# Sliding-window attention with V gathered for blocks of eight tokens, weights turned by DMA, and x loaded again in the new row order

## The chip, the cores and the metric

The kernel runs on one core of one Trainium2 chip. The metric is the device time of one execution in microseconds. A core has a matrix engine (TensorE, PE in the profile; its weight loads are PEld), a vector engine (VectorE, DVE), a scalar engine (ScalarE, ACT), GpSimd (POOL), and SyncE (SP), which here does nothing but issue DMAs. Each engine runs its own list of instructions in order; semaphores tie them together.

## The reference

One transformer block with adaptive layernorm on 2048 tokens of width 512 in bf16: attention over a dilated sliding window, then a gated FFN.

```python
mod = (silu(c) @ w_mod).reshape(1, 6, 1, -1)       # sa, ca, ga, sb, cb, gb
h = layernorm(x) * (1 + ca) + sa
x = x + ga * A(h, A_wqkv, A_wo)
h = layernorm(x) * (1 + cb) + sb
x = x + gb * B(h, B_w1, B_w3, B_w2)

def A(x, wqkv, wo):                                # S = 2048, D = 512, H = 32 heads of 16
    q, k, v = split(x @ wqkv)
    idx = arange(S)[:, None] - 2 * arange(8)[None, :]       # W = 8 keys, dilation 2
    logits = einsum('bhsd,bhswd->bhsw', q, k[idx]) * 16 ** -0.5   # idx < 0: -1e9
    o = einsum('bhsw,bhswd->bhsd', softmax(logits), v[idx])
    return o @ wo

def B(x, w1, w3, w2):                              # F = 1792
    return (silu(x @ w1) * (x @ w3)) @ w2
```

## The kernel before

The tokens are 16 tiles T of 128. A small program (`Program`) collects operations with their engine, what they read and write, and a key; two lists written into the file, `ORDER` and `SLOTS`, give the order of all operations and the buffer of every value. `place` splits the order into one list for each engine, `synchronize` works out the semaphores, `emit` writes the instructions. So each engine's order, SP's too, is fixed by `ORDER`, whose numbers count the calls of `p.op` and `p.dma` as `_build` makes them.

What is done, with the lines of the profile:

- Layernorm 1 in groups of tiles (0,1), (2,3), (4-7), (8-11), (12-15) on VectorE (L555, L576). The normalized tiles are turned by TensorE (L636) or, for the last two groups, by DMA (`sb_h<-sb_xn`), and scaled on ScalarE (L644, L621). Then q and k (L691) and v (L711) are projected. V is written to DRAM (`v_scratch_dram<-sb_v`) with its columns ordered by (channel, head).
- The modulation: `gate(0)` and `gate(1)` (L531, from `wm_g`) make ga and gb, which are multiplied into wo (L946) and w2 (L952).
- Attention in seven blocks of pairs of tiles (`BLOCKS`; the last has two pairs). `logits`: VectorE multiplies q with the eight shifted views of k (L742, called pq here), TensorE sums over the 16 channels of each head (L752, four column tiles of 32 at a time; tile 0 gets a mask, L749). `shift`, `exps`, `softmax`: maximum, subtraction, exponential, sum, reciprocal and scaling (L764, L769, L782, L794, L796, L797). The weights then have heads on the partitions. `turn` (L807) transposes them on TensorE into PSUM, and ScalarE copies them to SBUF (L811, `sb_al`), so that (token, offset) pairs lie on the partitions.
- `values`, for one tile: four DMAs of 256 KB copy V from DRAM so that partition 8 t + w of a copy holds the row of V of token t at offset w. Each row of V is so read eight times. VectorE multiplies the copy with the weights in place (L827, one instruction of 4096 elements a partition), TensorE sums over the eight offsets (L855), ScalarE copies the sum to SBUF (L861, `sb_ac`), a DMA transposes it (`sb_ot<-sb_ac`), TensorE multiplies with wo (L867), and VectorE adds the residual x (L871).
- The FFN in groups (0,1), (2,3), (4-7), (8-11), (12,13), (14,15). Layernorm 2 on GpSimd and ScalarE (L586 to L601), the turn by TensorE for the first two groups and by DMA for the others, then w1 and w3 (L883), silu (L889), the product (L892), w2 (L921; L909 for tiles 14 and 15), the last residual (L931) and the store (`out_dram<-sb_o`).

The FFN of one group runs between the attention of later pairs, in the order that the list gives.

Of the kernel before, what the change touches and what calls it, by code (L numbers as in the profile page):

```python
# [73 lines left out]
class Program:  # L74
# [41 lines left out]
    def dma(self, out, in_, key, packets, r=(), w=(), part=(), after=(), eng="sp", cost=450, group=None, transpose=False,  # L116
            store=False, again=False, lat=None):
# [11 lines left out]
        o = self.op(eng, fn, cost, key, r=r, w=w, part=part, after=after, dma=(each, ns, *(lat if lat else (900, 200) if store else (900, 500) if transpose else (1300, 600))))  # L129
# [119 lines left out]
C_PQ, C_RED, C_ACC = 2203, 455, 800  # L249
# [3 lines left out]
def c_mm(n):  # L253
    return n * 5 // 12 + 3

# [13 lines left out]
AC_OLD = ()  # L269
# [3 lines left out]
def _build(p, A_x, A_wqkv, A_wo, B_w1, B_w3, B_w2, c, w_mod, out):  # L273
# [4 lines left out]
    x_view = x2d.rearrange("(t p) d -> p t d", p=P)  # L278

# [10 lines left out]
    qb = [sb([P, KT, 512], bf, f"q{i}") for i in range(4)]  # L290
# [3 lines left out]
    vshb = [sb([P, 8, D], bf, f"vsh{i}") for i in range(2)]  # L294
    pqb = [sb([P, W, KT, P], bf, f"pq{i}") for i in range(2)]
    NSM = 3
    atb = [sb([P, 2, 32, W], bf, f"attn{i}") for i in range(NSM)]
    alb = [sb([P, 2, 8, H], bf, f"al{i}") for i in range(3)]
    mxb = [sb([P, 2, 32], f32, f"mx{i}") for i in range(NSM)]
    ssb = [sb([P, 2, 32], f32, f"ssum{i}") for i in range(NSM)]  # L300
    otb = [sb([P, KT, P], bf, f"ot{i}") for i in range(3)]
# [5 lines left out]
    ones = sb([P, 256], bf, "ones")  # L307
    ind = sb([P, 16], bf, "ind")
    ind2 = sb([P, 2, 32], bf, "ind2")
    before = sb([P, W, 2, 16], bf, "before")  # L310
# [26 lines left out]
    osb = [nc.alloc_sbuf_tensor_at(f"sb_o{i}", [P, D], bf, offset=nc.lookup_mloc(wqkv).addr + 8192 + 1024 * i) for i in range(4)]  # L337
    vsh_x = nc.alloc_sbuf_tensor_at("sb_vshx", [P, 8, D], bf, offset=nc.lookup_mloc(wqkv).addr)
# [12 lines left out]
    vshpool = Pool("vsh", vshb)  # L351
    pqpool = Pool("pq", pqb)
# [8 lines left out]
    def held(pool, items):  # L361

        vals = []
        for i, item in enumerate(items):
# [5 lines left out]
    qkv_hold = held(vshpool, [vsh_x]) + held(opool, osb)  # L370

    vind2 = Val("ind2")
# [16 lines left out]
                                           pattern=[[-W, 16]], channel_multiplier=1), 200, k, w=[vind])  # L389
    p.op("pool", lambda e: e.affine_select(out=ind[:], in_=ind[:], compare_op=ALU.is_ge, fill=0.0, base=W - 1,  # L390
                                           pattern=[[W, 16]], channel_multiplier=-1), 200, k, w=[vind])
    p.op("dve", lambda e: e.memset(ind2[:], 0.0), 80, k, w=[vind2])
    for y in range(2):
        p.op("dve", lambda e, y=y: e.tensor_copy(bass.AP(ind2, 33 * y, [[64, P], [2, 16]]), ind[:]), 150, k, r=[vind], w=[vind2])
    p.op("pool", lambda e: e.memset(before[:], 0.0), 250, k, w=[vbefore])
    p.op("pool", lambda e: e.affine_select(out=before[:], in_=before[:], compare_op=ALU.is_ge, fill=BEFORE, base=0,
                                           pattern=[[-DIL, W], [1, 2], [2, 16]], channel_multiplier=0), 400, k, w=[vbefore])
# [115 lines left out]
    def warm(i, after=()):  # L513

        vw = Val("ps_warm", psum)

        def mm(e):
            return e.matmul(bank(vw)[:, 0:256], ones[:, 0:P], ones[:], start=True, stop=True)

        p.op("pe", mm, 214, ("warm", i), r=[vc], w=[vw], after=after)  # L520
# [210 lines left out]
    def logits(Ts):  # L731

        vl = Val("ps_l", psum)
        for i, T in enumerate(Ts):
# [11 lines left out]
            def red(e, i=i, T=T, vp=vp):  # L746
                c0 = vl.at * 512 + i * W * 32
                if T == 0:
                    e.matmul(PALL[0:32, c0:c0 + W * 32], ones[:, 0:32], before[:], start=True, stop=False, tile_position=(0, 0))  # L749
                for ft in range(KT):  # L750
# [187 lines left out]
    for gi, Ts in enumerate(LN1):  # L938
# [4 lines left out]
        for i, T in enumerate(Ts):  # L943
            proj_v(T, i, vh)
# [10 lines left out]
    for groups in BLOCKS:  # L955
        vls = [logits(Ts) for Ts in groups]
        ves = [shift(Ts, vl) for Ts, vl in zip(groups, vls)]
        for Ts, vl, ve, vx_ in zip(groups, vls, ves, exps(groups, vls, ves)):
            val = softmax(Ts, vl, ve, vx_)
            for i, T in enumerate(Ts):  # L960
                values(T, i, val)
# [114 lines left out]
```

## Time and profile before

| | |
|---|---|
| median of 3 timed runs | 243.23 us (242.37 to 243.58) |
| the profiled execution | 242.82 us, span 241.1 us |
| granted TensorE clock | 1.00 |
| TensorE, VectorE, ScalarE, GpSimd busy | 230.4, 179.6, 138.7, 30.9 us |
| DMA | 38.85 MB in 46317 packets, of which the 64 copies of V 16.8 MB |
| issues on SP | 64 for V, 36 transposes, 18 output stores, 16 stores of v, the rest weights and x |

The span is what the profile covers; the 1.7 us between it and the execution's time lie around it. "Busy" counts a TensorE instruction until its modelled end, which overlaps the next one, so the start-to-start time of a run of matmuls says more than the mean of one. In the timeline a bracket at the end of a line is the idle time of that engine just before, and what ended it.

### The profile page before, as it was taken

The page shows a single profiled execution, that of the slowest core. Times are in us where ns is not written, and L with a number is a line of the kernel's source. Part 1 is how long each engine was busy: PE and PEld are TensorE (multiplying, and loading weights), DVE is VectorE, ACT ScalarE, POOL GpSimd, SP SyncE. Part 2 cuts the span into 40 slices and gives each one's busy share as a digit, 9 for nine tenths or more (in the row PEclk, how much of TensorE's full clock was granted, in tenths as well). Part 3 has the DMA queues.
Part 4 walks back from the last instruction along what each step waited for, and adds up shares of the span by engine and source line. Part 5 has one row for each costly group of instructions (what it writes and reads, how often), then busy time and mean ns, then how long its engine had stood idle before and what let it go on. Part 6 is the DMA issues. An engine that isn't in the chain of part 4 may idle for free.

```text
span 241.1 us, 4538 instructions
## 1 busy us (share of the span) xinstructions
PE 230.4 (96%) x1781; PEld 136.8 (57%) x1806; DVE 179.6 (75%) x279; ACT 138.7 (58%) x267; POOL 30.9 (13%) x66
## 2 busy tenths in 40 slices
PE   7988999979999999999799999999999999999995
PEld 4856454544587685564345444444565584485874
DVE  5697999979989999898999999764565044423542
ACT  2296497688999744955964578646537253140300
POOL 4332060004001000250005301001001000000000
PEclk9999999999999999999999999999999999999999
DMA  6999999999979996693893882253220300000103
GB/s 222 370 327 327 163 262 234 287 282 343 331 134 253 283 270 115 160 272 99 213 256 119 195 197 46 66 141 98 76 79 0 46 0 0 3 22 0 48 0 109
DMA packets 46317, 38.85 MB, mean 161 GB/s; under 512 B 21704, under 2 KB 37080, under 8 KB 46296
## 3 DMA queue, kind: packets, MB, share of 16 engines
q1 hardware_dynamic: 46288, 38.56, 62.5%
q8 instruction: 14, 0.23, 0.4%
q14 instruction: 7, 0.06, 0.1%
q10 hardware_dynamic: 8, 0.00, 0.0%
HBM read 29.62 MB, written 4.21 MB: 140 GB/s over the span
## 4 chain that ended last, share of the span: by engine, by line
PE 50%; ACT 1%; DMA 1%; issue 1%; DVE 0%; SPq 0%
PE pall L883 30%; PE pall L921 12%; PE pall L867 3%; PE pall L909 3%; DMA sb_h<-sb_xn 1%; ACT sb_h L621 1%; PE pall L855 1%; PE pall L752 1%; PE pall L807 0%; ACT sb_al L811 0%; DVE sb_o L931 0%; SPq L124 0%
## 5 line engine op out<-in xcount | busy, mean ns | idle before, releaser
L883 PE MATMUL pall<-sb_h,sb_w 128*128 128x256 bf16 (+1 forms) x665 | 101.8, 307 | 1.0 <-ACT sb_h L621 0.6
L883 PEld LDWEIGHTS pall<-sb_h,sb_w 128*128 128x128 bf16 x672 | 64.8, 98 | 36.2 <-issue 1.5
L892 DVE TENSOR_TENSOR sb_hh<-sb_sg,pall 128x256 bf16<-128x256 bf16 (+1 forms) x84 | 40.4, 505 | 32.1 <-PE pall L883 32.0
L889 ACT ACTIVATE sb_sg<-pall 128x256 bf16<-128x256 f32 (+1 forms) x84 | 36.2, 455 | 43.4 <-PE pall L883 37.3
L921 PE MATMUL pall<-sb_w,sb_hh 128*128 128x512 bf16 x189 | 43.7, 379 | 0.4
L742 DVE TENSOR_TENSOR sb_pq<-sb_q,sb_kT 128x4096 bf16<-128x4096 bf16 x16 | 36.3, 2282 | 0.0
L921 PEld LDWEIGHTS pall<-sb_w,sb_hh 128*128 128x128 bf16 x196 | 19.1, 98 | 21.0
L691 PE MATMUL pall<-sb_h,sb_wqkv 128*128 128x512 bf16 (+1 forms) x159 | 30.3, 336 | 0.1
L827 DVE TENSOR_TENSOR sb_vsh<-sb_vsh,sb_al 128x4096 bf16<-128x4096 bf16 x12 | 27.3, 2286 | 2.4 <-ACT sb_al L811 2.2
L621 ACT ACTIVATE sb_h<-sb_h,sb_modc 128x512 bf16<-128x512 bf16 (+1 forms) x24 | 16.3, 733 | 13.0 <-DMA sb_h<-sb_xn 13.0
L691 PEld LDWEIGHTS pall<-sb_h,sb_wqkv 128*128 128x128 bf16 x160 | 15.1, 98 | 12.2 <-ACT sb_h L644 0.5
L931 DVE TENSOR_TENSOR sb_o<-pall,sb_x 128x512 bf16<-128x512 f32 (+1 forms) x18 | 10.9, 627 | 11.8 <-PE pall L921 8.7
L586 POOL TENSOR_SCALAR sb_nm<-sb_sx 128x2 f32<-128x2 f32 x8 | 3.7, 465 | 115.9 <-DVE sb_x L871 115.9
L590 ACT ACTIVATE sb_xn<-sb_x,sb_nm 128x512 bf16<-128x512 bf16 x16 | 11.4, 714 | 11.7 <-POOL sb_nm L586 11.7
L867 PE MATMUL pall<-sb_wo,sb_ot 128*128 128x512 bf16 x60 | 15.0, 379 | 1.1 <-DMA sb_ot<-sb_ac 0.5
L711 PE MATMUL pall<-sb_wqkv,sb_h 128*128 128x512 bf16 x58 | 15.0, 379 | 0.3 <-issue 0.2
L644 ACT ACTIVATE sb_h<-pall,sb_modc 128x256 bf16<-128x256 bf16 (+1 forms) x18 | 9.9, 616 | 8.6 <-DVE sb_modc L509 6.7
L601 ACT ACTIVATE sb_xn<-sb_x,sb_nb,sb_rs 128x512 bf16<-128x512 bf16 x16 | 12.6, 806 | 3.7 <-POOL sb_nb L599 3.7
L871 DVE SCALAR_TENSOR_TENSOR sb_x<-pall,sb_x 128x512 bf16<-128x512 f32 x16 | 11.0, 688 | 2.3 <-PE pall L867 2.3
L701 ACT ACTIVATE sb_kT<-pall 128x512 bf16<-128x512 f32 x16 | 9.6, 606 | 4.7 <-PE pall L691 4.7
L555 DVE BATCH_NORM_STATS2 sb_st<-sb_x 128x6 f32<-128x512 bf16 x16 | 10.4, 678 | 1.3 <-DMA sb_x<-in_A_x_dram 1.3
L721 ACT ACTIVATE sb_v<-pall 128x512 bf16<-128x512 f32 x16 | 9.6, 612 | 2.4 <-DMA v_scratch_dram<-sb_v 2.3
(87 smaller groups left out, 208.6 us busy)
## 6 DMA issues: line engine op xcount, KB each, us to landing
sb_vsh<-v_scratch_dram SPq DMA_DIRECT2D x48, 256.0 KB, 4.6
sb_vshx<-v_scratch_dram SPq DMA_DIRECT2D x16, 256.0 KB, 4.3
sb_w<-in_B_w_dram SPq DMA_DIRECT2D x6, 512.0 KB, 5.6
sb_w<-in_B_w_dram SPq DMA_DIRECT2D x6, 384.0 KB, 6.0
v_scratch_dram<-sb_v SPq DMA_DIRECT2D x16, 128.0 KB, 5.9
out_dram<-sb_o SPq DMA_DIRECT2D x14, 128.0 KB, 1.9
sb_wqkv<-in_A_wqkv_dram SPq DMA_DIRECT2D x6, 256.0 KB, 6.0
sb_x<-in_A_x_dram SPq DMA_DIRECT2D x4, 256.0 KB, 6.3
```

Of the source, the lines that this page charges most:

```text
L590: p.op("act", lambda e, vn=vn, T=T: e.activation(vn.at[:], x_sb[:, T, :], ACT.Square, bias=nm[:, T, :], accum_out=var[:, T, :]), c_act(512 ...
L601: p.op("act", lambda e, vn=vn, T=T: e.activation(vn.at[:], x_sb[:, T, :], ACT.Identity, bias=nb[:, T, :], scale=rs[:, NT + T, :]), c_act(5 ...
L621: return e.activation(vh.at[:, ft, 0:n * P], vh.at[:, ft, 0:n * P], ACT.Identity, bias=modc[:, 8 * which + ft:8 * which + ft + 1], scale=m ...
L691: ins = e.matmul(bank(vp)[:, j * n:(j + 1) * n], wqkv[:, t, col:col + P], vh.at[:, t, 0:n], start=(t == ORDER[0] and j == 0), stop=(t == O ...
L711: ins = e.matmul(bank(vp), vh.at[:, t, tt * P:(tt + 1) * P], wqkv[:, t, 2 * D:3 * D], start=(t == ORDER[0]), stop=(t == ORDER[-1]))
L742: return e.tensor_tensor(vp.at[:], in0, in1, ALU.mult)
L827: return e.tensor_tensor(v_w, v_w, a_w, ALU.mult)
L867: ins = e.matmul(bank(vy), vt.at[:, ft, :], wo[:, ft, :], start=(ft == 0), stop=(ft == KT - 1))
L883: ins = e.matmul(bank(vp)[:, 0:n], wt[:, t, fi * P:(fi + 1) * P], vh.at[:, t, 0:n], start=(t == 0), stop=(t == KT - 1))
L889: p.op("act", lambda e: e.activation(vt.at[:, 0:n], bank(vgp)[:, 0:n], ACT.Silu), c_act(n), k, r=[vgp], w=[vt], table="silu")
L892: p.op("dve", lambda e: e.tensor_tensor(vh_.at[:, 0:n], vt.at[:, 0:n], bank(vup)[:, 0:n], ALU.mult), c_dve(n), k, r=[vt, vup], w=[vh_])
L921: ins = e.matmul(bank(vz), vhh[fi].at[:, tt * P:(tt + 1) * P], w2[:, fi, :], start=(fi == 0), stop=(fi == NF - 1))
```

## The change

The pairs of tiles are treated as one. The 256 tokens of a pair are 32 blocks of eight. The window of a token reaches back in steps of two, so the eight tokens of a block and their eight offsets need 22 rows of V, which five copies (`s`) of two neighbouring slots for four offsets (32 blocks x 4 offsets on the partitions) hold; each slot of a copy serves one token with its near four offsets and another with its far four. Five DMAs of 256 KB a pair take the place of eight. For this the logits are laid out with heads and the token's place in half a block (`q`) on the partitions, the scaling of the weights (`norm`) is written in two instructions, a DMA transpose takes the place of TensorE's turn and ScalarE's copy (`AT_PE` is empty), and the products are three instructions for 6, 2 and 8 slots, the first into a buffer of its own (`av`).

The sums come out with the tokens of a pair in another order: partition 32 q + j of half z is token 8 j + 4 z + q. So x is loaded a second time in that order, by 16 DMAs in two groups (`AGAIN`) over the rows that layernorm 1 has read; layernorm 2 and the FFN work on the new order, and each output tile is stored by four DMAs of 32 rows, or, for tiles 14 and 15, by one DMA for half the columns whose DRAM side has the dimensions 4, 32, 256. The three buffers of V copies for a tile become two for a pair; q has three buffers for four; the output has six buffers for four. `ORDER` and `SLOTS` are new as a whole.

```diff
+NQB = 3
+AT_PE = ()
+AGAIN = [[0, 1, 2, 3], [4, 5, 6, 7]]
+    def rows(t, T, x, n_pairs, c0=0, n=D):
+        first = T // 2 * 2 * P + T % 2 * 4 + x
+        return bass.AP(t.tensor, t.offset + first * D + c0, [[8 * D, 32]] + ([[2 * P * D, n_pairs]] if n_pairs > 1 else []) + [[1, n]])
...
-    vshb = [sb([P, 8, D], bf, f"vsh{i}") for i in range(2)]
+    vshb = [sb([P, 10, D], bf, f"vsh{i}") for i in range(2)]
+    avb = [sb([P, 6, D], bf, "av0")]
...
             def red(e, i=i, T=T, vp=vp):
+                def group(q):
+                    return PALL[32 * q:32 * q + 32, vl.at * 512:vl.at * 512 + 512].rearrange("p (w n r) -> p w n r", w=W, n=2)[:, :, i, :]
...
-                        ins = e.matmul(PALL[32 * q:32 * q + 32, c0:c0 + W * 32], E_sb[:, ft, :], bass.AP(vp.at, ft * P + 32 * q, [[W * KT * P, P], [KT * P, W], [1, 2], [2, 16]]),
-                                       start=(ft == 0 and (T > 0 or q > 0)), stop=(ft == KT - 1), tile_position=(0, 32 * q))
+                        ins = e.matmul(group(q), E_sb[:, ft, :], bass.AP(vp.at, ft * P + q, [[W * KT * P, P], [KT * P, W], [4, 32]]),
+                                       start=(ft == 0), stop=(ft == KT - 1), tile_position=(0, 32 * q))
...
-        p.op("dve", lambda e: e.tensor_tensor(ve.at[0][:, 0:n], bass.AP(PALL, bank(vl).offset, [[8 * 512, P], [W * 32, n], [1, 32], [32, W]]),
-                                              bass.AP(ve.at[2], 0, [[64, P], [32, n], [1, 32], [0, W]]), ALU.mult),
+        for y in range(2):
+            def norm(e, y=y):
+                return e.tensor_tensor(bass.AP(ve.at[0], y * P, [[512, P], [256, 2], [4, 32], [1, 4]]),
+                                       bass.AP(PALL, bank(vl).offset + y, [[8 * 512, P], [64, 2], [2, 32], [128, 4]]),
+                                       bass.AP(ve.at[2], y, [[64, P], [0, 2], [2, 32], [0, 4]]), ALU.mult)
+            p.op("dve", norm, 74 + 267, k, r=[vr, vx_], part=[va], hold=[ve, vl], lock=False)
+        val = Val("al", alpool)
+        if Ts[0] not in AT_PE:
+            p.dma(lambda: val.at[:], lambda: ve.at[0][:], ("at", Ts[0]), (128, 1024), r=[va], w=[val], hold=[ve], cost=1270, transpose=True)
+            return val
...
-        for q in range(4):
-            p.dma(lambda q=q: vv.at[:, 2 * q:2 * q + 2, :],
-                  bass.AP(v_dram, (PAD + T * P + 32 * q) * D, [[2 * D, 16], [-DIL * D, W], [1, 2 * D]]), ("vl", T), (128, 2048),
+        for s in range(5):
+            p.dma(lambda s=s: vv.at[:, 2 * s:2 * s + 2, :],
+                  bass.AP(v_dram, (PAD + T0 * P - DIL + 2 * s) * D, [[8 * D, 32], [-2 * DIL * D, 4], [1, 2 * D]]), ("vl", T0), (128, 2048),
...
-        avs[T] = p.op("dve", av, C_PQ, ("av", T), r=[val], w=[vv], lock=True)
+        first = p.op("dve", av(1, 2, 6, 2, vpr, 0), c_av(6), k, r=[val, vin], w=[vhigh], hold=[vv, vpr], lock=True)
+        p.op("dve", av(1, 0, 2, 0, vv, 0), c_av(2), k, r=[val, vin], part=[vlow], hold=[vv], lock=True)
+        o = p.op("dve", av(0, 0, 8, 2, vv, 2), c_av(8), k, r=[val, vin], part=[vlow], hold=[vv, vpr], lock=True)
...
+        if T >= NT - 2:
+            first = T // 2 * 2 * P + T % 2 * 4
+            finals.append(p.dma(bass.AP(out2d.tensor, out2d.offset + first * D + c0, [[D, 4], [8 * D, 32], [1, n]]), lambda: vo.at[:, 0:n], ("zo", T), (128, 2 * n),
+                                r=[vo], cost=400, store=True))
+            return
+        parts = []
+        for x in range(4):
+            finals.append(p.dma(rows(out2d, T, x, 1, c0, n), lambda x=x: vo.at[32 * x:32 * x + 32, 0:n], ("zo", T), (32, 2 * n), r=[vo], cost=400, store=True, group=parts))
...
+    for g, prs in enumerate(AGAIN):
+        loads = []
+        for z in range(2):
+            Ts = [2 * pr + z for pr in prs]
+            for x in range(4):
+                p.dma(x_sb[32 * x:32 * x + 32, Ts[0]:Ts[-1] + 1:2, :], rows(x2d, Ts[0], x, len(Ts)), ("again", g), (32 * len(Ts), 1024),
+                      part=[vx[T] for T in Ts], group=loads, cost=500)
```

Numbering the operations gives the lists in words. SP from the first store of v to the second output transpose ("vl" a copy of V, "st" a store of v, "hT" a transpose for sb_h, "OT" one for sb_ot, "AT" the one of the weights, "X" a load of x of the first group, "w" a weight):

```
before: st1 st0 w hT8 st2 hT10 w vl0 hT9 hT11 vl0 vl0 vl0 st3 vl1 vl1 vl1 st4 vl1 w hT14 hT12 st6 w st11 hT13 hT15 w w OT0 OT1
after:  X st3 st1 X st0 hT8 hT9 w X hT10 hT11 st7 vl0 hT14 vl0 vl0 vl0 vl0 st6 AT0 w st2 w st5 hT13 w X hT15 hT12 X X OT1 X OT0 (then X)
```

VectorE between the reciprocal and the first products of the first pair: before, xn12, xn13, the scaling, pq3, xn15; after, a copy for the modulation, the two halves of the scaling, xn12, xn13, pq2, xn15. TensorE ahead of the first gate and between the gates: before, three transposed pieces of tiles 4 to 7, gate 0, the other pieces and three projections, gate 1; after, all eight pieces, gate 0, eight projections, gate 1. The projection of v of tile 12 lies ahead of the first FFN matmul before, and behind it after.

## The prediction

> **What bounds the kernel now.** I read the page first: busy shares and the 40 slices.
>
> ```profile
> PE 230.4 (96%) x1781; PEld 136.8 (57%) x1806; DVE 179.6 (75%) x279; ACT 138.7 (58%) x267; POOL 30.9 (13%) x66
> PE   7988999979999999999799999999999999999995
> DVE  5697999979989999898999999764565044423542
> DMA  6999999999979996693893882253220300000103
> ```
>
> TensorE is busy almost throughout, VectorE for some 125 us in the middle, the DMA engines for the first 70 us. Busy time overstates TensorE, so the second view is the chain that ended last, in order of time.
>
> ```profile
> 110.83 2.44 DMA sb_h<-sb_xn
> 113.29 2.94 ACT sb_h L621 x4
> 116.50 5.99 PE pall L883 x27
> 232.34 6.13 PE pall L909 x56
> 238.49 0.42 DVE sb_o L931
> ```
>
> (Most of its pieces are left out.) From 116.5 us to the end everything on the chain is TensorE at its issue rate (56 matmuls of 256 columns in 6.13 us, 109 ns each). Behind 116.5 us only TensorE work counts; ahead of it TensorE waits for data. So the third view is TensorE's timeline up to there, for its gaps and for what fills it while the first pair of tiles passes through attention.
>
> ```profile
> 18.10 0.54 PE L531 MATMUL pall<-sb_csT_bf,sb_wm_g 128*128 128x1 bf16 x16 [0.63 <-DMA sb_wm_g<-in_w_mod_dram]
> 22.71 0.54 PE L531 MATMUL pall<-sb_csT_bf,sb_wm_g 128*128 128x1 bf16 x16 [0.88 <-DMA sb_wm_g<-in_w_mod_dram]
> 36.77 0.39 PE L807 MATMUL pall<-sb_ident,sb_attn 128*128 128x128 bf16 x4
> 50.99 1.67 PE L867 MATMUL pall<-sb_wo,sb_ot 128*128 128x512 bf16 x7 [0.46 <-ACT sb_h L621]
> 62.20 1.89 PE L691 MATMUL pall<-sb_h,sb_wqkv 128*128 128x512 bf16 x8
> 63.93 1.47 PE L883 MATMUL pall<-sb_h,sb_w 128*128 128x256 bf16 x12
> ```
>
> The last projection (L691) ends just as the first FFN matmul (L883, 63.93 us) can start. Up to there the projections are the only filler; when they are used up, TensorE waits for the first pair's chain: weights (L797), turn (L807), copy (L811), products (L827), column sums (L855), output transpose by DMA, WO (L867), residual (L871), second layernorm, FFN. A delay in this chain that the filler doesn't cover is a delay of the end.
>
> **The change, part by part.** All sums are against the profiled execution, 242.82 us (span 241.1 and 1.7 around it); the median of the timed runs, 243.23, is 0.4 above it, and runs spread from 242.37 to 243.58. About 0.5%, 1.2 us, is what a measurement can tell from no change.
>
> *TensorE.* The turn goes: four transposes take 0.22 us of the queue (the next piece starts at 37.00 after 36.77), eight groups 1.8 us. Two groups lie ahead of the first FFN matmul, six (1.3 us) behind it. The logit and column-sum matmuls keep their number and columns. The mask for tile 0 becomes four matmuls of 32 columns in place of one of 256: under 0.1 us either way.
>
> *ScalarE, GpSimd, buffers.* Eight copies of the turned weights go (L811, 598 ns): 4.8 us on an engine that is 58% busy; what counts is the wait ahead of the products, below. GpSimd builds the mask in five instructions for two (0.2 to 0.6 us each), before tile 0 needs it at 29 us: nothing. Three q buffers for four: the fourth chunk is written from some 50 us on, when the first chunk's last product (at 36.20 us now) is over: nothing.
>
> *VectorE.* The scaling L797 is split in two, the products of a pair become three instructions for two. Four 256-column L892 in a row took 1.41 us, so one adds 0.33; two L797 in a row took 1.22, so one of 512 adds 0.54 to 0.61. Two halves cost about 0.09 more than one; an extra instruction's fixed part, by the same two rows, is 0.08. Eight pairs: 8 x 0.17 = 1.4 us on an engine that is full from 30 to 155 us. After that it idles and TensorE has a stock of FFN work, so I cost this at nothing on the end; if the third FFN group (116.5 us) waits for it, half of it, 0.7 us, shows.
>
> *DMA and SP.* 24 copies of 256 KB go (6.3 MB); 2.1 MB of x and eight transposes come. On SP: 24 x 0.62 us less (four issues took 2.45), 8 x 1.25 us for transposes, 16 x 0.58 for x, 42 more output stores at 0.33 to 0.41: some 20 us more on SP, most of it behind 100 us, where SP waits for VectorE anyhow. Ahead of 50 us SP is full, though, and numbering the operations as the code makes them, the new order list has there five copies of V for eight, plus one transpose and seven of the eight loads of x ahead of the second output transpose: 3 x 0.62 less, 1.25 + 7 x 0.58 more, 3.4 us; two weight loads moved behind them give 1.2 back. So +2.2 us on SP, hidden at least in part: of the 30.5 us from 17.75 to 48.2, SP issued for 26.0. The eighth load of x is issued behind both output transposes, and the residual of tile 0 waits for all eight. On SP the weights' transpose waits for L797, with weight loads, stores of v and the transposes of tiles 12 to 15 behind it, which the layernorm of these tiles fed earlier.
>
> *The first pair's chain.* Now: weights done at 36.28 (35.60 + 0.68), turned and copied by 37.80, products from 38.72, with one logit product in between. New: a DMA transpose. No row has this one, the nearest are those of the same window:
>
> ```profile
> sb_vsh<-v_scratch_dram SPq DMA_DIRECT2D x8, 256.0 KB, 5.1
> sb_h<-sb_xn SPq DMA_TRANSPOSE x4, 6.1
> sb_ot<-sb_ac SPq DMA_TRANSPOSE x2, 4.5
> ```
>
> (Issues from 30 to 50 us, last column median us from issue to landing.) So 4.5 to 6.1 us where turn and copy took 1.5. Two xn instructions (0.33 each) now lie behind the weights, so these are done at about 35.7 and landed at 40.2 to 41.8: the products start 1.5 to 3.1 us later, with VectorE standing still, and pq of tiles 4 and 5, the scaling of wo and everything else of VectorE queued behind. The residual's wait for x adds 0 to 1. What gives back: less DMA traffic ahead (three copies of V and two weight loads, against 1 MB of x), and slack in the chain, which the rows bound at 0 to 2 us (ScalarE stood 0.33 and 0.85 us in the layernorm waiting on GpSimd, the rest is queueing). Ends: 0 and 3.5 us; I take 1.5, below the middle since the queue will be shorter. The two waits of the gates (0.63 + 0.88 us) will go, since the list puts five more pairs of transposes ahead of the first gate and five more projections between the two; with the chain as the limit that only empties the filler sooner, so nothing.
>
> *Behind the first FFN matmul.* 1.3 us of turns go; the list moves one projection of V (v12, four matmuls, 0.86 us) there. -0.45 us.
>
> *The tail.* The last stores now write rows as 4 x 32 x 512 B by one DMA. Stores of this size landed 1.5 us after issue:
>
> ```profile
> DMA to landing us min/median/max: 1.5/1.6/1.8
> ```
>
> Bounds: no change; or, if only four engines carry it, 32 packets each in place of 8, at most at the mean packet of the page (0.625 x 16 x 241.1 us / 46288 = 52 ns), 1.25 us. Packets here are 512 B against a mean of 833, so I take half, 0.6. [...]
>
> Sum: 1.5 - 0.45 + 0.6 = +1.65 us, 244.5 by the profiled execution, 244.9 by the median: I say 244.7.
>
> **The rivals.**
>
> *Faster: TensorE sets all of it.* If the weights land by the time the logit product ends (38.7 us), the chain is not longer, and 1.8 us of turns and the gates' 1.5 us of waits come off: 242.82 - 3.3 + 0.6 = 240.1, by the median 240.5. It decides at a landing under 3 us. For it: TensorE's 96%; later transposes landed in 2.4 to 2.8 us where the DMA engines were half idle; the order is new as a whole and may use the freed engines better than my reading of one chain. Against: 4.5 to 6.1 us in that window. 0.33.
>
> *No change.* The chain is longer by under a microsecond, and what TensorE saves pays for it: 1.2 us around 243.2. 0.17.
>
> *More than one stall.* The third FFN group is late as well: VectorE's 1.4 us and the first pair's stall reach 113 us, where TensorE already stood 0.67 and 0.55 us, and 4-part stores sit between the transposes of sb_h on SP. 2 to 3 us more: 247.5. 0.10.
>
> *The logit matmuls slow down.* They now read pq at a step of four elements, not two, and write PSUM in runs of 32 with gaps. 256 of them at 27 ns (16 in 0.44 us): at half speed +7 us, 251. A row speaks against the gaps: the turn wrote runs of 32 and took as long as the layernorm's transposes into whole rows.
>
> ```profile
> L636 PE MATMUL pall<-sb_ident,sb_xn 128*128 128x128 bf16 x48 | 4.2, 219 | 0.1
> L807 PE MATMUL pall<-sb_ident,sb_attn 128*128 128x128 bf16 x32 | 3.1, 219 | 0.2 <-ACT sb_sg L889 0.2
> ```
>
> [...] 0.03.
>
> **How the numbers follow.** The forecast (a longer first chain, one stall) has 0.37, slower by over 0.5%; with the last two rivals, 0.50 slower; 0.17 within 0.5%; 0.33 faster. The range leaves out the slow matmuls, the worst of two stalls and the best of the faster case: 239.8 to 248.0. The forecast's own range, by its bounds (chain 0.5 to 3.5, tail 0 to 1.25), is 243.3 to 247.
>
> **What would show it.** Right: VectorE idle 1.5 to 3 us ahead of the first product with a DMA of sb_al as releaser, the first L883-type matmul at 65 to 66 us with TensorE idle just before, and the last store landing 2 us or more after issue. Wrong: the weights' transpose landing in under 3 us, the first FFN matmul at 62 to 63 us, and the span shorter by what the turns and gates held. Also wrong: a logit matmul spacing above 30 ns, or a new gap behind 116 us, where I expect none.

## The result, and the profile after

The changed kernel takes 249.06 us (median of 4 runs, 248.92 to 249.59), the kernel before beside it 242.96 (242.37 to 243.58): a ratio of 1.0255, 95% interval 1.0223 to 1.0287. It is slower, as forecast, but by 6.1 us and not by 1.5, and it lies above the range. The profiled execution took 248.92 us, its span is 247.2. Of the kernels further down, five executions took over 1.5% longer than the fastest of the same kernel (244.32, 253.43, 255.96, 256.73 and 261.28 us); the times given are medians of all runs, the ratios leave these five out.

First the page of the changed kernel: busy time, and the slices.

```profile
PE 237.6 (96%) x1777; PEld 136.4 (55%) x1777; DVE 180.5 (73%) x292; ACT 134.7 (55%) x259; POOL 27.4 (11%) x69
PE   7998999999999999979999999999999999999994
DVE  5698889989879999969989979996255332513531
DMA  6999998979998993694287460423122000001002
```

The change took 32 transposes off TensorE, and TensorE is busy 7.2 us longer (25 of its records are missing from the trace of before: PE x1781 for PEld x1806; so a little less in truth). ScalarE has 4.0 us less, VectorE 0.9 more. The DMA engines move 35.72 MB for 38.85, in more packets (50142 for 46317).

The chain that ended last, in order of time, has a line on it that was no part of the forecast:

```profile
49.61 1.94 PE pall L764 x29
...
111.34 6.22 PE pall L935 x28
118.54 1.85 PE pall L764 x27
120.39 12.19 PE pall L897 x56
...
237.71 6.13 PE pall L923 x56
```

L764 are the logit matmuls, 1.85 us of the chain just ahead of the third FFN group, where the chain of before had none (some records are missing, so the count says 27 for 32). The groups of instructions, before and after, ahead of the bar matrix shape and count, behind it busy time, mean ns of one and idle time:

```profile
L752 PE MATMUL pall<-sb_pq,sb_E 128*32 128x256 bf16 x256 | 9.1, 271 | 0.9 <-ACT sb_kT L701 0.9
```
```profile
L764 PE MATMUL pall<-sb_pq,sb_E 128*32 128x256 bf16 x256 | 16.5, 405 | 0.0
```

As many matmuls, of the same shape. The mean of one overstates them (four run side by side); their spacing comes from start to start in TensorE's timeline, up to the column sums (L855, now L868) behind them. Before:

```profile
42.27 0.62 PE L752 MATMUL pall<-sb_pq,sb_E 128*32 128x256 bf16 x16
42.72 0.60 PE L855 MATMUL pall<-sb_vsh,sb_ind 128*32 128x512 bf16 x8
```

After, with the marks that are used below:

```profile
65.16 2.78 PE L897 MATMUL pall<-sb_h,sb_w 128*128 128x256 bf16 x24
...
92.24 1.09 PE L764 MATMUL pall<-sb_pq,sb_E 128*32 128x256 bf16 x16
93.14 0.41 PE L868 MATMUL pall<-sb_vsh,sb_ind 128*32 128x512 bf16 x4
...
111.34 6.22 PE L935 MATMUL pall<-sb_w,sb_hh 128*128 128x512 bf16 x28 [1.56 <-DVE sb_hh L906]
...
118.37 2.02 PE L764 MATMUL pall<-sb_pq,sb_E 128*32 128x256 bf16 x32
120.32 12.26 PE L897 MATMUL pall<-sb_h,sb_w 128*128 128x512 bf16 x56
```

16 matmuls held the queue for 0.45 us before (42.27 to 42.72, 28 ns each) and for 0.90 after (92.24 to 93.14, 56 each): 28 ns more, 7.2 us for 256, as the busy times of the two rows say too (16.5 - 9.1 = 7.4 us). From 118.37 to 120.32, with full-width matmuls behind, it is 61 ns each; but there 32 matmuls with the reads of before take 31 ns each as well (e1_read2 below, 117.09 to 118.08 us). The 33 ns and 8.6 us in the expectations below set 61 against 28 and are too large. The marks of the two kernels give the time by stretches: first FFN matmul 63.93 to 65.16 us (+1.2), third FFN group 116.50 to 120.32 (+2.6 more), end of TensorE's work 238.47 to 243.84 (+1.55 more), from there to the end of the span 2.63 to 3.36 (+0.7).

And the step that the forecast hung on, the weights' transpose by DMA, as the issues from 30 to 50 us show it (last column median us from issue to landing):

```profile
sb_h<-sb_xn SPq DMA_TRANSPOSE x4, 4.3
sb_ot<-sb_ac SPq DMA_TRANSPOSE x2, 3.1
sb_al<-sb_attn SPq DMA_TRANSPOSE x1, 2.3
```

It landed in 2.3 us. The products started at 39.34 us (38.72 before), with no wait ahead of them.

### The profile page after: what moved, and what is told of

Read it like the earlier page. It is cut to its first block, busy times and chain, and to the rows that moved or that the text cites. A ratio compares the mean times of both kernels' runs of the same rounds, so it can differ in the third digit from the quotient of the medians.

```text
span 247.2 us, 4554 instructions
## 1 busy us (share of the span) xinstructions
PE 237.6 (96%) x1777; PEld 136.4 (55%) x1777; DVE 180.5 (73%) x292; ACT 134.7 (55%) x259; POOL 27.4 (11%) x69
## 2 busy tenths in 40 slices
DMA packets 50142, 35.72 MB, mean 144 GB/s; under 512 B 26552, under 2 KB 43976, under 8 KB 50120
## 4 chain that ended last, share of the span: by engine, by line
PE 71%; DMA 10%; ACT 10%; SPq 4%; POOL 2%; DVE 2%; issue 1%; DVEq 0%
PE pall L897 35%; PE pall L935 12%; PE pall L700 5%; PE pall L764 5%; PE pall L881 5%; DMA sb_wm_g<-in_w_mod_dram 4%; SPq L124 4%; DMA sb_h<-sb_xn 3%; PE pall L868 3%; PE pall L923 2%; ACT sb_h L630 2%; PE pall L720 2%; ACT sb_xn L610 2%; DMA sb_ot<-sb_ac 2%; ACT sb_xn L599 2%
## 5 line engine op out<-in xcount | busy, mean ns | idle before, releaser
L903 ACT ACTIVATE sb_sg<-pall 128x256 bf16<-128x256 f32 (+1 forms) x84 | 35.6, 454 | 55.6 <-PE pall L897 54.7
L935 PE MATMUL pall<-sb_w,sb_hh 128*128 128x512 bf16 x196 | 44.6, 379 | 1.6 <-DVE sb_hh L906 1.6
L751 DVE TENSOR_TENSOR sb_pq<-sb_q,sb_kT 128x4096 bf16<-128x4096 bf16 x16 | 36.3, 2286 | 3.9 <-PE pall L764 2.8
L700 PE MATMUL pall<-sb_h,sb_wqkv 128*128 128x512 bf16 (+1 forms) x160 | 31.0, 337 | 0.7 <-ACT sb_h L630 0.6
L848 DVE TENSOR_TENSOR sb_vsh<-sb_vsh,sb_al 128x1024 bf16<-128x1024 bf16 (+1 forms) x16 | 23.5, 1485 | 0.5 <-DMA sb_al<-sb_attn 0.4
L700 PEld LDWEIGHTS pall<-sb_h,sb_wqkv 128*128 128x128 bf16 x160 | 15.0, 98 | 13.2 <-DVE sb_ssum L808 1.1
L720 PE MATMUL pall<-sb_wqkv,sb_h 128*128 128x512 bf16 x64 | 16.5, 379 | 0.0
L764 PE MATMUL pall<-sb_pq,sb_E 128*32 128x256 bf16 x256 | 16.5, 405 | 0.0
L881 PE MATMUL pall<-sb_wo,sb_ot 128*128 128x512 bf16 x64 | 15.8, 379 | 0.3 <-DMA sb_ot<-sb_ac 0.3
L873 ACT ACTIVATE sb_ac<-pall 128x512 bf16<-128x512 f32 x16 | 8.9, 594 | 5.9 <-PE pall L868 5.9
```

Of the source, the lines that this page charges most:

```text
L700: ins = e.matmul(bank(vp)[:, j * n:(j + 1) * n], wqkv[:, t, col:col + P], vh.at[:, t, 0:n], start=(t == ORDER[0] and j == 0), stop=(t == O ...
L720: ins = e.matmul(bank(vp), vh.at[:, t, tt * P:(tt + 1) * P], wqkv[:, t, 2 * D:3 * D], start=(t == ORDER[0]), stop=(t == ORDER[-1]))
L751: return e.tensor_tensor(vp.at[:], in0, in1, ALU.mult)
L764: ins = e.matmul(group(q), E_sb[:, ft, :], bass.AP(vp.at, ft * P + q, [[W * KT * P, P], [KT * P, W], [4, 32]]), start=(ft == 0), stop=(ft ...
L848: return e.tensor_tensor(o_w, v_w, a_w, ALU.mult)
L881: ins = e.matmul(bank(vy), vt.at[:, ft, n * P:(n + 1) * P], wo[:, ft, :], start=(ft == 0), stop=(ft == KT - 1))
```

## The experiments

The theory after the result (S): TensorE reads the products pq at a step of four elements, and that alone makes the logit matmuls slow. First rival (G): the gaps in the PSUM writes do it. Second rival (C): the matmuls are only a symptom, and the rest of the change (order list, loads, stores) costs the time. In the first three kernels the logits belong to other tokens than they should; the amount of work is the same. The edits are shortened: of a long line only the part that changes is shown.

**e1_read2**: the changed kernel with the reads of before; the gaps stay.

```diff
-  bass.AP(vp.at, ft * P + q, [[W * KT * P, P], [KT * P, W], [4, 32]])
+  bass.AP(vp.at, ft * P + 32 * q, [[W * KT * P, P], [KT * P, W], [1, 2], [2, 16]])
```

> The kernel after, but the logit matmuls (L764) read pq as the kernel before does (step of two elements, 32 tokens in two halves), and still write PSUM in runs of 32 with gaps; the logits so belong to other tokens. Theory S (the read step of four elements halves these matmuls): spacing back from 61 to 27 or 28 ns, 256 matmuls x 33 ns = 8.6 us off TensorE, time about 240.5 us, below the kernel before. Theory G (the gaps in the PSUM writes do it): spacing 61 ns, 249 us. Theory C (the matmuls are slower but hidden; the new chain or the new order costs the time): spacing 27 ns and the time stays within 2 us of 249.

**e2_dense**: the changed kernel, reads at step four, but PSUM written without gaps.

```diff
-  e.matmul(group(q), E_sb[:, ft, :], ...)
+  e.matmul(PALL[32*q:32*q+32, vl.at*512+i*W*32:vl.at*512+(i+1)*W*32], E_sb[:, ft, :], ...)
```

> The kernel after, with the read step of four kept and the PSUM writes of the logit matmuls dense, 256 neighbouring columns for a tile, as before (the softmax so reads other logits). S: spacing 61 ns, 249 us. G: spacing 27 ns, 240.5 us. C: as for e1_read2.

**e3_before_read4**: the kernel before, with nothing but the reads at step four.

```diff
-  bass.AP(vp.at, ft * P + 32 * q, [[W * KT * P, P], [KT * P, W], [1, 2], [2, 16]])
+  bass.AP(vp.at, ft * P + q, [[W * KT * P, P], [KT * P, W], [4, 32]])
```

> The kernel before with one change, the logit matmuls (L752) read pq at a step of four elements; its logits so belong to other tokens. S: spacing from 28 to 61 ns, up to 8.6 us more on TensorE, 250 to 252 us: as slow as the kernel after or slower. G and C: no change, 243 us.

Measured: 244.94 us (ratio to before 1.0094, 1.0059 to 1.0128), 249.74 (1.0263, 1.0213 to 1.0313) and 247.54 (1.0184, 1.0150 to 1.0217). The groups of the three kernels, in this order:

```profile
L764 PE MATMUL pall<-sb_pq,sb_E 128*32 128x256 bf16 x256 | 8.8, 271 | 0.0
```
```profile
L764 PE MATMUL pall<-sb_pq,sb_E 128*32 128x256 bf16 x256 | 16.4, 405 | 0.0
```
```profile
L752 PE MATMUL pall<-sb_pq,sb_E 128*32 128x256 bf16 x256 | 16.6, 405 | 0.0
```

Reads at step two with gaps: fast. Reads at step four without gaps: slow. One changed access pattern in the kernel before: slow, and 4.8 us later. S holds, G falls, and so does C as the whole story. But S had put e1_read2 at 240.5 us and e3_before_read4 at 250 to 252, so it counted too much. 244.94 is 2.2 us above before: the reads are worth 4.1 us of the 6.1 and not all of it. Of their 7.4 us of TensorE work some 3 disappear in waits that TensorE has anyhow: without them the first FFN matmul comes 0.8 us sooner (64.38 for 65.16), the third FFN group 2.2 (118.08), the end of TensorE's work 4.0 (239.85).

**e4_map**: the kernel before, with another pattern of reads (or writes) for each pair of tiles (one execution, 245.76 us); a map of what TensorE pays for.

```diff
+  pair = T // 2
+  tail, off = {0: ([[1, 2], [2, 16]], 32*q), 1: ([[1, 32]], 32*q), 2: ([[4, 32]], q), 3: ([[1, 2], [2, 16]], 32*q),
+               4: ([[3, 32]], q), 5: ([[8, 16], [1, 2]], 2*q), 6: ([[1, 2], [8, 16]], 2*q), 7: ([[2, 32]], q%2 + 64*(q//2))}[pair]
+  # pair 3: PSUM in runs of 32 with gaps
```

> The kernel before, where the logit matmuls of each pair of tiles read or write pq in another pattern (the logits so belong to other tokens); one look, spacings from the trace. Pair 0: as before. Pair 1: step 1, 32 in a row. Pair 2: step 4. Pair 3: as before, but PSUM writes in runs of 32 with gaps. Pair 4: step 3. Pair 5: two neighbours, then a jump of 8 elements. Pair 6: step 8. Pair 7: step 2, 32 in a run. [...] G: only pair 3 at 61.

TensorE's timeline, one line for a pair or a tile (pairs 1, 2, first half of 3, 4, 5, first half of 6, 7):

```profile
42.02 0.62 PE L766 MATMUL pall<-sb_pq,sb_E 128*32 128x256 bf16 x16
...
49.15 2.02 PE L766 MATMUL pall<-sb_pq,sb_E 128*32 128x256 bf16 x32 [0.79 <-ACT sb_kT L701]
...
66.18 0.62 PE L766 MATMUL pall<-sb_pq,sb_E 128*32 128x256 bf16 x16
...
92.17 1.69 PE L766 MATMUL pall<-sb_pq,sb_E 128*32 128x256 bf16 x32
...
113.77 2.01 PE L766 MATMUL pall<-sb_pq,sb_E 128*32 128x256 bf16 x32
...
131.44 2.00 PE L766 MATMUL pall<-sb_pq,sb_E 128*32 128x256 bf16 x16
...
140.47 1.08 PE L766 MATMUL pall<-sb_pq,sb_E 128*32 128x256 bf16 x32
```

16 in 0.62 and 32 in 1.08 are the full rate of 28 ns (a run's last matmul counts until its modelled end, some 0.17 us more than its turn in the queue). Step 1 and step 2 are free, and so are gaps of 32 fp32 values between runs of 32 in PSUM (pair 3, 16 in 0.62). Step 3 costs 48 ns a matmul, step 4 58, step 8 114 (16 in 2.00). Pair 5 decides what is counted: it reads two neighbours and then jumps by eight, so half its steps are 1, and it costs as much as step 4. What both have in common is two values out of each 16 bytes. Four of these matmuls run side by side, so one stream takes 4 x 58 = 232 ns for 256 columns in 128 stretches of 16 bytes at step 4, and 4 x 114 = 456 ns for 256 stretches at step 8: 1.8 ns for each 16 bytes newly touched, where the full rate is 4 x 28 / 256 = 0.44 ns a column. So 16 bytes cost nothing extra once they give four values (28 ns at step 2), and more with some 2.7 (48 ns at step 3: 4 x 48 = 192 ns for 96 stretches, 2.0 ns each). The 16 bytes, a line in the expectations below, are only a way of counting: stretches of 32 bytes at twice the price would give the same times up to step 8. Stretches of 8 bytes don't fit, since pair 5 would then touch half as many as pair 2 (step 4), and 32 matmuls took 2.01 and 2.02 us.

**f5_ffn_step**: is this special to the small matmuls in column tiles? The kernel before, with w1 reading `sb_h` at a step of 4, 8 or 2 in some groups.

```diff
-  ins = e.matmul(bank(vp)[:, 0:n], wt[...], vh.at[:, t, 0:n], start=(t == 0),
+  src = vh.at[:, t, 0:n];  s = (4, 8, 2, 3, 4, 1)[gi]
+  if wt is w1 and s > 1 and s != 3:
+      src = src.rearrange("p (a b) -> p b a", b=s)
+  ins = e.matmul(bank(vp)[:, 0:n], wt[...], src, start=(t == 0),
```

> The kernel before, where the w1 matmuls of the FFN (full width, one at a time) read sb_h at another step: group 0 at 4 elements, group 1 at 8, group 2 at 2, group 4 at 4 (tokens so in another order; w3 as before). One look: start to start of 256 columns is 109 ns. If the step slows any matmul as it slows the logit matmuls: 240 ns in groups 0 and 4, 470 in group 1. If it is the four logit matmuls running side by side that share the reads: 109 ns everywhere.

One execution, 278.82 us, at a granted clock of 0.957; at 115.08 us eight column sums took 1.04 us, for 0.61 at 89.81, but around the matmuls below seven of L925 took 1.67 (128.45 and 136.56 us), as they did at 90.81. From TensorE's timeline, w1 at step 8 and w3 at step 1, each four matmuls (with their modelled end):

```profile
119.14 1.97 PE L887 MATMUL pall<-sb_h,sb_w 128*128 128x256 bf16 x4
...
138.07 0.60 PE L887 MATMUL pall<-sb_h,sb_w 128*128 128x256 bf16 x4
```

Less the 0.16 us of the modelled end that the usual four show (0.60 for 4 x 109 ns), step 8 takes 0.45 us for one of 256 columns, four times the 109 ns: 1.8 ns for each 16 bytes again. The starts in the trace say the same: 0.45 us from one to the next at step 8 (four from 123.56 to 125.34 us), 0.23 at step 4 (the group at 65.68 us), 0.11 at step 1. So it isn't special to four small matmuls side by side: full-width ones pay it for their moving operand too.

**f4_e1_lean**: where the other 2.2 us are. e1_read2 without the 16 second loads of x (the residual so adds other rows) and with one store of 128 rows for each output tile (for tiles 14 and 15, one for each half of the columns).

```diff
-  for g, prs in enumerate(AGAIN): ...            # the 16 loads
-  for x in range(4): finals.append(p.dma(rows(out2d, T, x, 1, c0, n), ...))
+  finals.append(p.dma(out2d[T * P:(T + 1) * P, c0:c0 + n], lambda: vo.at[:, 0:n], ...))
```

> The kernel after with the read step of before (as e1_read2) and without the second loads of x (the residual so adds other rows) and with one dense store for each output tile (the rows so stand in another order). If these transfers are what is left of the loss: 0.8 us at the end (the stores of tiles 14 and 15 over 16 engines again) and the rest elsewhere, 242.5 to 243. If only the end is due to them and the rest is the new order of instructions: 244.1, with the first FFN matmul still near 64.4 and the third group's near 118.

Measured: 241.62 us, ratio 0.9938 (0.9919 to 0.9958), faster than before by 1.3 us and below the 242.5 to 243 expected; since it leaves out transfers that the result needs, this is a bound and not a repair. The first FFN matmul and the third group came 1.8 us sooner than in e1_read2, the end of TensorE's work 2.4, and the tail is 0.8 shorter:

```profile
62.55 2.78 PE L897 MATMUL pall<-sb_h,sb_w 128*128 128x256 bf16 x24
...
116.24 12.03 PE L897 MATMUL pall<-sb_h,sb_w 128*128 128x512 bf16 x54 [0.16 <-ACT sb_ac L873]
...
231.17 6.28 PE L923 MATMUL pall<-sb_w,sb_hh 128*128 128x256 bf16 x56
```

So the second loads cost some 1.8 us ahead of the first FFN matmul, where no output is stored yet, and the stores some 0.8 at the very end. The place of the loads' cost shows in the issues on SP of e1_read2:

```profile
42.58 0.58 SPq L124 DMA_DIRECT2D sb_x<-in_A_x_dram  x1
43.21 2.54 SPq L124 DMA_TRANSPOSE sb_h<-sb_xn  x2
45.80 1.06 SPq L124 DMA_DIRECT2D sb_x<-in_A_x_dram  x2
46.90 1.19 SPq L124 DMA_TRANSPOSE sb_ot<-sb_ac  x1
48.13 0.59 SPq L124 DMA_DIRECT2D sb_x<-in_A_x_dram  x1
48.76 1.23 SPq L124 DMA_TRANSPOSE sb_ot<-sb_ac  x1
50.04 0.58 SPq L124 DMA_DIRECT2D sb_x<-in_A_x_dram  x1
```

in its chain that ended last:

```profile
44.48 2.99 DMA sb_h<-sb_xn
...
50.49 1.04 PE pall L700 x4
51.53 1.73 PE pall L881 x8
```

and in its waits of VectorE from 50 to 54 us:

```profile
DVE sb_x L885 <- DMA sb_x<-in_A_x_dram: 0.9, 1, 0.9
```

Without the loads SP issued these two transposes for sb_h from 40.83 us on, and both output transposes were out by 47.92 us (49.99 with them). Two things end close together: WO (L881), in TensorE's order behind a projection (L700) that comes from one of these transposes, began at 51.37 us (49.65 without the loads), and the eighth load let the residual of tile 0 start at 52.90 (51.08). Both stand on SP behind loads of x. How the 1.8 us divides between them no run shows.

**f3_before_at**: does a DMA transpose on the first pair's chain hurt at all? The kernel before in its old order, with the weights turned by DMA; for this the products of a tile are two instructions for one.

```diff
-  p.op("pe", turn, ...);  p.op("act", ..., ACT.Copy, ...)
+  p.dma(lambda: val.at[:], lambda: ve.at[0][:], ("at", Ts[0]), ..., transpose=True)
```

> One part of the change alone: the kernel before, its order kept, with the weights turned by a DMA transpose issued right behind their scaling, in place of TensorE's turn and ScalarE's copy; the products of a tile are two instructions for one (the transposed weights have another order), the logit matmuls stay as they were. If the turn by DMA is what the change gains: 8 x 0.22 = 1.8 us off TensorE, of which the 1.3 us behind the first FFN matmul show: 241.3 to 242.3. If the landing of the transpose delays the first pair (my forecast's reason): first FFN matmul 1 us or more later than 63.9 and 243.5 to 245.

Measured: 256.88 us, ratio 1.0576 (1.0537 to 1.0616), at a granted clock of 0.98. VectorE's timeline:

```profile
44.19 4.63 DVE L817 TENSOR_TENSOR sb_vsh<-sb_vsh,sb_al 128x2048 bf16<-128x2048 bf16 x4 [5.53 <-DMA sb_al<-sb_attn]
```

The transpose was issued only at 38.69 us, behind two transposes for sb_h that held SP from 36.06 to 38.65, and landed 5.5 us later. This is the stall that the prediction described, 5.5 us and not 1.5 to 3.1; the first FFN matmul came at 69.34 us (63.93). Not all of these 5.4 us are the stall by itself: TensorE stood idle for 4.07 us up to 46.61, and right behind that its matmuls were slower (16 logit matmuls 1.07 us at 47.44, for 0.62 at 41.92). Of the 13.9 us that the whole kernel lost, far more than the 0.5 to 2 expected, the 8.5 behind this mark were not traced. In the changed kernel the new order issues the transpose at 36.28 with nothing of the kind right ahead, and the stall is gone.

**g4_e1_latex, g8_parity, g10_parity_latex**: two ways to mend. `latex`: the three earliest second loads of x moved behind the weights' transpose on SP. `parity`: ScalarE writes q and k with even and odd tokens apart, so that pq has two halves of 64 tokens and the matmuls read every second element, four to each 16 bytes (the address of q, the output of the product and the padding of k change likewise).

```diff
 # parity
-  dst = kT[:, f0:f0+m, PAD+512*cch+at0 : ...+n]
+  dst = bass.AP(kT, f0*(PAD+S) + (PAD+512*cch+at0)//2, [[KT*(PAD+S), P], [PAD+S, m], [(PAD+S)//2, 2], [1, n//2]])
-  in1 = bass.AP(kT, PAD + T*P, [[KT*(PAD+S), P], [-DIL, W], [PAD+S, KT], [1, P]])
+  in1 = bass.AP(kT, (PAD + T*P)//2, [[KT*(PAD+S), P], [-DIL//2, W], [(PAD+S)//2, 2*KT], [1, 64]])
-  bass.AP(vp.at, ft*P + q, [[W*KT*P, P], [KT*P, W], [4, 32]])
+  bass.AP(vp.at, ft*P + q%2*64 + q//2, [[W*KT*P, P], [KT*P, W], [2, 32]])
```

> The changed kernel with the logit matmuls reading at step two (as in the first experiment, 244.94 us, first FFN matmul at 64.38 us), and in the order list the three earliest of the second loads of x moved from ahead of the first copies of V to just behind the transpose of the weights. Taking all second loads of x away had brought the first FFN matmul to 62.55. Theory A (the early loads hold up the transposes for sb_h on SP and on the DMA engines): first FFN matmul at 62.6 to 63.3, 243.5 us. Theory B (what costs is that the residual waits for the last of the eight loads, wherever they stand): 244.9 or, since the loads now come later still, up to 1 us more.

> [...] By the law of the pattern runs (full rate from four values a line) the 256 logit matmuls take 9.1 us as in the kernel before and the time is that of the first experiment, 244.9 us, if the product on VectorE stays at 2.29 us for one of 4096 elements and the copies of q and k on ScalarE at 0.60 us. [...] Second rival: the matmul's cost goes by the step in some way that the same pattern in the earlier runs didn't show: 249.

> Both edits at once in the changed kernel, complete: even and odd tokens apart, and the three early second loads of x behind the transpose of the weights. If both theories hold, 243.5 us, within 0.5% of the kernel before; if only the law of the lines holds, 244.9; if the late loads delay the residual, 245 to 246.

Measured: 245.78 us (1.0109, 1.0069 to 1.0149), 245.87 (1.0108, 1.0067 to 1.0149) and 246.34 (1.0132, 1.0086 to 1.0179). g8_parity came out 1 us above the 244.9 expected. Even and odd apart does what the pattern runs say, in a kernel that leaves nothing out; the groups:

```profile
L764 PE MATMUL pall<-sb_pq,sb_E 128*32 128x256 bf16 x256 | 8.9, 272 | 0.0
L751 DVE TENSOR_TENSOR sb_pq<-sb_q,sb_kT 128x4096 bf16<-128x4096 bf16 x16 | 36.9, 2319 | 1.2 <-ACT sb_q L709 0.8 <-PE pall L764 0.4
```

The matmuls are as fast as before the change, and the shift by one element costs VectorE 33 ns in 2286. Moving the loads gained nothing: the first FFN matmul came at 64.51 us in g4_e1_latex, where 62.6 to 63.3 was expected, and at 65.75 in g10_parity_latex. But theory A, that early loads hold up the transposes, isn't refuted by it, for the loads went from one part of SP's queue into another, still ahead of the last transposes for sb_h. In g4_e1_latex the weights were scaled at 34.09 us (35.59 in e1_read2); then their transpose, now with three loads right behind it, landed in 3.9 us for 2.3, the last two transposes for sb_h were issued from 43.34 (43.21), and the residual waited 1.50 us for the eighth load, until 53.03 (52.90). What was gained early was lost by there, as theory B said. In g10_parity_latex the weights' transpose landed in 3.5 us, and the output transposes were issued at 47.81 and 49.67, a microsecond later than in g8_parity.

**h1_parity_pool, h2_parity_pool_tail**: parity, with the second loads of x issued by GpSimd; h2 also splits the very last store in four over two queues.

```diff
-  part=[vx[T] for T in Ts], group=loads, cost=500)
+  part=[vx[T] for T in Ts], group=loads, cost=500, eng="pool")
 # h2, last half tile only
+  for x in range(4): p.dma(rows(out2d, T, x, 1, c0, n), ..., eng="act" if x > 1 else "sp")
```

> The changed kernel, complete, with even and odd tokens of q and k apart (245.9 us by itself), and all 16 second loads of x issued by GpSimd's queue instead of SP's. GpSimd stood idle from 23 to 35 us and from 36 to 55 us in the changed kernel. Moving three of the loads later on SP gained nothing; so theory A is that their issue time on SP (8 x 0.58 us ahead of the second output transpose) is what costs: first FFN matmul at 62.6 to 63.0 (with no loads at all it was 62.55), 244.0 us. Theory B, that their traffic or the residual's wait for the last of them costs, leaves 64.4 and 245.9, or later if GpSimd's loads take longer to land. Rival C: GpSimd's issues take 1 us or more each and hold up the layernorm's steps on GpSimd (0.7 us each): first FFN matmul past 65, over 246.5 us.

> The same, and the very last store (32 KB more than half of which was still moving 0.75 us after issue) split into four DMAs of 32 rows, two from SP's queue and two from ScalarE's. Time from the end of the last addition to the end of the span 2.9 us in the changed kernel, 2.19 before the change. If the single DMA with the split row dimension is what made the tail longer, 0.4 to 0.7 us less than the other kernel of this call, 243.4 us; if what costs is the count of issues or rows of 512 bytes in scattered places, the same time as the other.

Measured: 248.27 us (1.0211, 1.0174 to 1.0247) and 249.62 (1.0243, 1.0214 to 1.0271), both slower than with the loads on SP. GpSimd issues quickly (five in 2.85 us from 36.43 us in h2), so rival C falls, and so does theory A in its second form: it isn't SP's time alone (two transposes for sb_h now held SP for 4.62 us from 42.85, for 2.54 in g8_parity). These five are issued around the weights' transpose (36.69). Issues from 30 to 52 us in h2, and VectorE's timeline:

```profile
sb_x<-in_A_x_dram POOLq DMA_DIRECT2D x5, 128.0 KB, 5.4
sb_h<-sb_xn SPq DMA_TRANSPOSE x4, 5.9
...
sb_al<-sb_attn SPq DMA_TRANSPOSE x1, 4.7
```
```profile
41.45 1.76 DVE L848 TENSOR_TENSOR sb_av<-sb_vsh,sb_al 128x3072 bf16<-128x3072 bf16 x1 [1.58 <-DMA sb_al<-sb_attn]
```

The transpose takes 4.7 us, VectorE stands 1.58 us: what the prediction expected of the change itself. The landing went with the traffic that is let out around it: 2.3 us in the changed kernel and in g8_parity; 4.7 in h2_parity_pool_tail, which up to there differs from g8_parity only in where the loads of x are issued, five of them beside the transpose (in both it was issued 3.0 us behind the last copy of V). The others had more than one thing changed: 3.5 and 3.9 with three loads behind it, but issued 1.9 us behind the last copy of V; 3.9 in f4_e1_lean, without any load of x, but issued 1.4 us behind that copy. The split last store brought 0.3 us at most, for 0.4 to 0.7 expected (2.64 us from the last addition to the end of the span, 2.92 in the changed kernel); the two medians, 248.27 and 249.62 us, differ the other way, within the spread of their runs, and don't show it.

No version here that leaves nothing out beats the kernel before. To keep the 241.62 us of f4_e1_lean the sums of the attention would have to come out in natural order, so that the second loads and the split stores go; that wasn't tried.

## Why the prediction was right or wrong

**Slower, but out of the range.** The rival "the logit matmuls slow down" is what happened, and it stood at 0.03. Its price, +7 us and 251, was near (249.06); the chance was wrong. The step that failed is the row set against it: that the turn (L807) and the layernorm's transposes (L636) took 219 ns alike. Both read whole rows of 128 columns at a step of one, and differ in what they write. So they spoke against the gaps, which indeed cost nothing, and were silent on the reads at a step of four, which the same sentence named first. No row shown had such a read: nothing on record stood behind the 0.03, and the sum put the term at nothing; it measured 7.2 to 7.4 us of TensorE work and 4.1 us of time. The prediction's own sign of being wrong, a logit matmul spacing above 30 ns, came true at 56 ns. The cost had to be kept in the range from 0 to 7 us.

**The chain of the first pair.** Taken at +1.5 us through a landing of 4.5 to 6.1 us; it landed in 2.3, the products started 0.6 us later, with no wait. f3_before_at and h2_parity_pool_tail show that such a stall exists, but in the changed kernel there was none: the landing went with the neighbours in the queue and on the engines, and the rows that it was taken from (transposes in the old order, with eight copies of V around) were the wrong neighbours. (The prediction gives the lower end of this term once as 0 and once, for its own range, as 0.5 us; the landing speaks for 0.) The mark "first FFN matmul at 65 to 66 us" came true at 65.16 by luck, for other reasons: the logit reads (0.8) and the loads of x (1.8), less what the new order without loads gains (62.55 against 63.93, -1.4).

**SP's 2.2 us and the wait for x.** "Hidden at least in part" and 0 to 1 us. The loads cost about 1.8 us: the transposes for sb_h and sb_ot queued behind them on SP, and the residual waited for the eighth load (0.9 us in e1_read2). This term was too small, and it was the larger cost in the chain.

**What TensorE saves.** The faster rival counted 3.3 us off TensorE. With reads and loads taken out and stores whole, f4_e1_lean came to -1.3 us: that much the core of the change and its new order list are worth together. Of the gates' waits, 0.63 and 0.88 us, which "will go", one is gone and the other is there as 1.03 us at 19.18. The landing under 3 us, at which that rival was to decide, came; it didn't decide, because the loads and the reads lay behind it.

**Behind the first FFN matmul.** Taken at -0.45 us, it was +2.6 up to the third FFN group: the slow reads of six tiles (6 x 16 x 28 ns = 2.7 us, partly in waits; without them e1_read2 came 1.5 us nearer), and the gap of 1.56 us at 111.34, where TensorE waited for the product behind silu and where before it stood 0.67 and 0.55. This gap stayed at 1.55 to 1.59 us in every kernel with the new order, f4_e1_lean too, so it goes with the list; it wasn't tried by itself, and the rest of the 2.6 wasn't taken apart.

**The tail.** +0.6 forecast, +0.7 measured (2.63 to 3.36 us from TensorE's end), in the upper half of the bounds. No run up to then showed a store carried by four engines; the 0.6 was the author's estimate, half of what that would cost at the mean packet. The DMA engines in the last 5 us of the changed kernel, in 40 slices, and in the last of the kernel before, from 237 us on:

```profile
DMA  3000012222232223221022222220000000000000
GB/s 90 8 0 0 0 33 45 74 86 82 86 90 86 82 86 94 82 82 41 4 49 61 86 90 86 86 62 0 0 0 0 0 0 0 0 0 0 0 0 0
```
```profile
DMA  9459300000781000000000592000000000000000
GB/s 328 123 156 287 82 0 0 0 0 4 225 254 41 0 0 0 0 0 0 0 0 0 168 279 78 0 0 0 0 0 0 0 0 0 0 0 0 0 0 0
```

A store of 64 KB moves at 80 to 90 GB/s for most of a microsecond with two to three tenths of the 16 engines busy, which is about four engines; before, the last one went at up to 279 GB/s in three of these slices, some 0.4 us, with up to nine tenths busy. The trace agrees with four, and f4_e1_lean, with one block of rows to a store, had the shorter tail back (2.5 us).

**VectorE** was near: +0.9 us busy for +1.4 estimated, and nothing of it on the end that the runs show.

## What to carry to other kernels

When a layout is changed to save transfers, write down the innermost step of every matmul's moving operand: here each 16 bytes newly touched cost about 1.8 ns (2.0 at step 3), so that with under four bf16 values in 16 bytes the matmul slowed: from 28 ns to 48, 58 and 114 at steps of 3, 4 and 8 in column tiles of 32, and from 109 ns to 0.23 and 0.45 us at steps of 4 and 8 in full width. The cure can lie one step upstream, where an engine writes the operand anyway; sorting even from odd tokens cost VectorE 33 ns a product (2319 for 2286). And a DMA moved onto a chain need not take what it took elsewhere (here 2.3 to 5.5 us): ask which transfers are issued in the two or three microseconds before and after it, and bound it by those.

A row clears a suspect only if it has the property in question on the same side, read or write.

## What was not expected of the hardware

- TensorE's moving reads in e4_map: 28 ns a matmul (four side by side, 256 columns) at a step of 1 or 2, 48 at 3, 58 at 4, 114 at 8; two neighbours and a jump cost as much as step 4. Gaps in PSUM, in runs of 32 fp32, cost nothing (e4_map, pair 3: 0.62 us for 16).
- VectorE multiplied bf16 at nearly the same speed with half of the shifted views of k an odd number of elements (of 2 bytes) away from q: 2319 ns a product in g8_parity, 2286 in the changed kernel, where all shifts are even.
- One DMA transpose of the same 128 KB landed in 2.3 to 5.5 us, with different transfers around it; with five loads beside it, it was 4.7 for 2.3.
